# Splitting the late loads of v from those of q and k, and replacing the written order of engines and banks, in a fused attention and feed-forward kernel

## The chip, the cores and the metric

The kernel runs on one core of a Trainium2 chip. The metric is the device time of the program in microseconds (us); lower is better. The kernel before takes 197.51 us, the median of three runs (197.26 to 197.86).

## The reference

The inputs are q, k and v of shape (4 batches, 8 heads, 768 positions, 64), and two weights, w_in (512 x 2048) and w_out (2048 x 512). Attention keeps, for each query, the first 8 positions ("global") and the last 96 ("local"), with a distance penalty whose slope goes with the head. The result is laid out as 3072 tokens of 512 and goes through a feed-forward layer.

```
rel = pos[:, None] - pos[None, :]
keep = (pos[None, :] < 8) | ((rel >= 0) & (rel < 96))
scores = where(keep, q @ k.T / sqrt(64) - slope * dist, -1e9)
x = softmax(scores) @ v            # to (3072, 512)
out = relu(x @ w_in) ** 2 @ w_out  # (3072, 512), f32
```

## The kernel before

The tokens are cut into 24 tiles j of 128 rows (6 for each batch), and pairs of tiles form 12 blocks of 256 rows. A token tile goes through attention: q and k are transposed so that the head dimension lies on partitions (operations tr and T), the bias and the scores are made in PSUM (bias L597, sc L618), ScalarE takes exponentials (exp L684), VectorE multiplies them by a mask of decays (mul L709), TensorE multiplies with v, which carries a column of ones for the sum (pv L767), and VectorE divides by that sum (norm, a reciprocal at L797 and a product at L798). The first rows of k and v of a batch serve all its tiles; small copies, gk and gv (L455 on VectorE, L453 on ScalarE), put them where the next tile reads them. So x is made tile by tile, and then transposed: for the first 8 tiles by TensorE and a copy (trx L835, xT), for the other 16 by a transposing DMA on SP's queue (L859). Tiles 8 and up also have their q and k transposed by such DMAs (T.j on SP).

The feed-forward layer works on blocks. Block 0 and half of block 1 take the plain product (s1 L1081), with relu (L884 or L886) and square (sq). From there on each 256-row block and each half g of w_in uses a scheme of seven products in place of eight (h.blk.g.p1 to p7, L967): differences of x (xs, L939) and sums of w_in (isum, L907) feed it, ScalarE copies four of the results out of PSUM (u, L453), a custom VectorE instruction adds a PSUM bank to such a copy and clips at zero (c, L1011; c21 is a plain clip, L884 or L886), and a square follows (q, L1031 on ScalarE or L1033 on VectorE). The second layer has the same scheme: sums of the squared tiles (sum, L1185) and of w_out (wsum, L1150), seven products (s2.blk.p1 to p7, L1230), copies of parts (part), sums of two outputs of 128x256 (o, L1305), and stores (st, L1327, SP's queue).

All inputs come by DMAs that GpSimd's queue (POOL) issues: the first tiles of q, k and v and the weights one by one (ld.q.j, ld.k.j, ld.v.j, ld.win, ld.wout, L330), and tiles 6 to 23 as one operation load.j, which issues v, q and k in this order (L334). A load of tile j reuses a slot of a ring: v has 10 slots, q and k have 6 that hold the first tiles and 3 further ones. A load may start when the last readers of its slot are done; a tiny memset by VectorE (gate.j) passes on some of these waits.

Nothing in the kernel chooses the order at run time or at build time: the class Plan records every operation with its dependences, and its method run gives them out in the order of a long string, ORDER. A word of it is the name of an operation, #n for its n-th instance, @A or @V for ScalarE or VectorE where either can do it, and after a colon the PSUM banks (0 to 7), or the buffers of a ring, that it takes. Each engine, and each DMA queue, gets its instructions in this order, and semaphores are added where a dependence crosses engines. So the string fixes which operation stands behind which on each engine.

Of the kernel before, what the change touches and what calls it, by code (L numbers as in the profile page):

```python
# [57 lines left out]
tr.0.0:0 T.0.0@V tr.1.0:1 bias.0.0:23 T.1.0@V ld.q.1 ld.k.1 tr.0.1:4 T.0.1@V ld.q.2 ld.k.2 E0.1 ld.q.3 ld.v.0 ld.k.3  # L58
tr.1.1:5 T.1.1@A ld.v.1 sc.0.0 bias.1.0:6701 exp.0.1.0:0 sc.1.0 tr.0.2:4 exp.0.0.0 gk.1@A T.0.2@V exp.1.0.0:1 tr.1.2:5
T.1.2@V bias.2.0:3264 sc.2.0 exp.1.1.0 exp.1.1.1:3 ld.k.4 exp.1.0.1 ld.q.4 pv.0.1:5 tr.0.3:7 pv.0.0:1 ld.v.2 gk.2@A  # L60
exp.2.1.1:4 exp.2.0.0:5 exp.2.0.1 exp.2.1.0 tr.1.3:0 T.0.3@V T.1.3@V sc.3.0:4730 norm.0.0:0 norm.0.1 pv.1.0:6 tr.1.4:1
ld.q.5 pv.1.1:2 norm.1.0:1 norm.1.1 trx.0:5 exp.3.1.1:6 ld.k.5 gv.1@A ld.v.3 tr.0.4:0 T.1.4@V T.0.4@V xT.0@A:0 gk.3@V
trx.1:6 exp.3.0.1 exp.3.1.0:7 exp.3.0.0 ld.win.1.0 pv.2.0:2 pv.2.1:5 norm.2.0:0 norm.2.1 gv.2@V mul.3.0:8 sc.4.0:1037
exp.4.1.0:9 trx.2:2 ld.win.4.0 xT.1@A exp.4.1.1:a tr.1.5:4 tr.0.5:5 T.1.5@A exp.4.0.0 xT.2@A:1 mul.3.1:b pv.3.0:0
pv.3.1:6 T.0.5@A s1.0.1:7 norm.3.0:1 gk.4@V exp.4.0.1 norm.3.1 gv.3@A s1.0.1#2 trx.3:4 sc.5.0:0126 exp.5.0.1:c
exp.5.1.0:d s1.0.4:5 exp.5.1.1 E0.0 mul.4.0:e xT.3@V ld.v.4 mul.4.1:f ones.6 pv.4.0:3 s1.1.1:4 relu.0.4@V:2 exp.5.0.0
ld.win.3.0 s1.0.3:2 pv.4.1:1 relu.0.1@A:0 sq.0.1@A:0 gv.4@A s1.0.3#2 mul.5.1:1 s1.1.3:6 norm.4.0:0 norm.4.1 ld.win.2.0
ld.win.0.0 s1.0.0:5 relu.0.3@A:3 sq.0.3@A mul.5.0:5 gate.10 s1.0.2:0 trx.4:7 relu.1.1@A:4 sq.1.1@A:1 xs.1.0:0 ld.v.5
ld.win.2.1 pv.5.0:3 ld.win.0.1 pv.5.1:1 xs.1.1 ld.win.6.0 ld.win.7.0 ld.win.5.0 relu.1.3@A:7 norm.5.0:1 norm.5.1
ld.wout.3 s1.1.2:2 xT.4@A:2 relu.1.2@A:8 ld.wout.2 ld.wout.1 ld.wout.0 isum.0.0 s1.1.0:4 s1.0.2#2 trx.5:3 gate.14  # L70
xT.5@V relu.1.0@A:6 sq.1.2@A s1.0.0#2 xs.2.0:1 h.2.0.p1:1 sq.1.0@V sq.0.4@A u.2.0.1@A:b isum.3.0 sq.1.3@A xs.2.1
ld.wout.7 isum.0.1 s1.0.0#3 s1.0.6:6 gate.11 isum.1.0 isum.1.1 xs.1.2 s1.0.7:7 h.2.0.p2:2 c.2.0.c11:9 h.2.1.p1:3
relu.0.6@A:a ld.wout.6 ld.wout.5 ld.wout.4 u.2.1.1@A:e relu.0.7@A:c isum.3.1 s1.0.0#4 h.2.1.p5:4 s1.0.2#3 relu.0.0@A:f
h.1.1.p1:6 h.2.1.p2:7 u.1.1.1@A:0 isum.2.1 h.2.1.p6 u.2.1.2@A:d h.1.1.p2:2 c.1.1.c11:3 xs.2.2 c.2.1.c11:5 sq.0.0@A
s1.0.2#4 isum.2.0 h.1.1.p6 u.1.1.2@A:1 h.2.0.p6 u.2.0.2@A:4 h.2.1.p7 u.2.1.3@A:8 h.1.1.p7 h.2.0.p5:5 relu.0.2@A:6
u.1.1.3@A:2 h.2.0.p7 wsum.0.0 h.1.1.p5:2 u.2.0.3@A:7 c.2.1.c22:b wsum.1.0 sq.0.2@A gate.9 s1.0.5:7 h.2.1.p3 wsum.2.0
c.2.0.c22:f load.6 load.7 c.1.1.c22:0 sq.0.7@A relu.0.5@A:e sq.0.6@A sq.0.5@A load.8 c.2.1.c12:8 sum.0.2:0 sum.0.0
h.1.1.p4 h.2.0.p4 wsum.0.1 s2.1.p1.0:0 T.8 c.2.0.c21@A:6 h.2.0.p3 h.2.1.p4 s2.0.p1.0:7 h.1.1.p3 sum.0.1 s2.0.p2.0:4
q.1.1.c22@A q.1.1.c11@A s2.0.p1.1 q.2.1.c22@A:2 q.2.0.c11@A part.0.p1@A:0 c.1.1.c21@A:c s2.0.p2.1 s2.1.p1.1 wsum.1.1
s2.0.p6.0 s2.0.p6.1 c.1.1.c12:7 tr.1.6:1 tr.0.6:6 part.1.p1@A:1 q.1.1.c21@A s2.1.p2.0:2 q.2.1.c11@A sum.0.3 wsum.2.1  # L80
part.0.p6@A:2 o.0.p2:a c.2.1.c21@A:2 s2.1.p2.1 wsum.3.1 wsum.3.0 T.1.6@V s2.0.p7.0 s2.0.p7.1 gate.12 s2.0.p5.0
q.1.1.c12@A s2.0.p5.1 c.2.0.c12:e load.9 part.0.p7@A:3 q.2.1.c12@A T.0.6@A q.2.0.c22@A o.0.p5:d s2.0.p4.0 s2.0.p4.1
q.2.0.c12@A o.0.p4@A sum.1.0:1 s2.0.p3.0 tr.0.7:3 gate.13 sum.1.1 s2.0.p3.1 o.1.p2:0 o.0.p3 sum.1.2 T.0.7@A tr.1.7:1
sum.2.2:0 sum.1.3 sum.2.0 T.1.7@A q.2.0.c21@A s2.1.p6.0 s2.1.p6.1 q.2.1.c21@A part.1.p6@A:0 sc.6.0:567341 exp.6.1.0:3
load.10 gk.7@A exp.6.0.0 s2.1.p5.0 s2.1.p7.0 s2.1.p7.1 mul.6.0:b exp.7.0.0:9 exp.7.1.0 part.1.p7@A:3 s2.2.p1.0:6
s2.1.p5.1 sum.2.1 exp.7.0.1:1 exp.7.1.1 o.1.p5:c mul.7.0:5 s2.2.p1.1 pv.6.0:5 norm.6.0:0 s2.1.p4.0 s2.1.p4.1 o.1.p4@A
pv.6.1:7 s2.1.p3.0 sc.8.0:3415 exp.8.0.1:7 part.2.p1@A:1 pv.7.0:0 s2.1.p3.1 mul.7.1:8 norm.6.1 T.9 pv.7.1:7 norm.7.0:1
# [5 lines left out]
part.2.p7@A:3 q.3.0.c11@A h.3.0.p5:2 h.3.1.p2:1 c.3.1.c11:8 gv.8@V load.11 c.3.0.c22:7 h.3.1.p3 h.3.0.p4 c.3.0.c21@A:2
h.3.1.p4 c.3.1.c21@A:1 q.3.1.c11@A c.3.1.c12:6 s2.2.p5.0 pv.9.0:5 gk.9@V T.11 st.0.0 norm.9.0:1 q.3.1.c12@A
q.3.0.c22@A h.3.0.p3 pv.9.1:1 gv.9@A c.3.0.c12:e norm.9.1 s2.3.p1.0:0 s2.2.p5.1 sc.10.0:4752 exp.10.1.1:f h.4.0.p1:1
s2.2.p4.0 exp.10.1.0:3 s2.2.p4.1 q.3.0.c12@V s2.3.p1.1 sum.3.0:1 o.2.p5:b s2.2.p3.0 s2.2.p3.1 exp.10.0.1 exp.10.0.0
part.3.p1@A:0 sum.3.1 h.4.1.p1:2 s2.3.p6.0 o.2.p4@A mul.10.0:8 s2.3.p6.1 sum.3.2 pv.10.0:7 mul.10.1:9 o.2.p3 gk.10@A
xT.9 norm.10.0:0 xs.4.0:1 xs.4.1 h.4.1.p2:5 pv.10.1:4 q.3.1.c21@A q.3.0.c21@A part.3.p6@A:1 u.4.1.1@A:6 u.4.0.1@A:5
s2.3.p7.0 s2.3.p7.1 h.4.1.p6 u.4.1.2@A:7 norm.10.1 h.4.0.p6 u.4.0.2@A:e gate.18 sc.11.0:6374 exp.11.1.0:a exp.11.0.0
gv.10@V c.4.1.c11:3 part.3.p7@V:3 sum.3.3 xs.4.2 load.12 h.4.0.p2:5 T.12 exp.11.1.1:1 h.4.1.p7 s2.3.p4.0 mul.11.0:2  # L100
exp.11.0.1 c.4.0.c11:f u.4.1.3@A:8 mul.11.1:9 load.13 h.4.0.p7 h.4.1.p5:3 c.4.1.c22:6 s2.3.p2.0:6 pv.11.0:4
u.4.0.3@A:a norm.11.0:1 q.4.1.c11@A:1 h.4.1.p4 h.4.0.p5:7 c.4.0.c22:5 s2.3.p2.1 o.3.p2:2 pv.11.1:5 q.4.1.c22@A
h.4.1.p3 q.4.0.c11@A gate.16 norm.11.1 h.4.0.p4 c.4.1.c21@A:1 c.4.0.c21@A:3 h.4.0.p3 s2.3.p4.1 c.4.1.c12:8 q.4.1.c12@A
# [69 lines left out]
def kernel(  # L173
# [37 lines left out]
    NBIAS = 3  # L211
    JQK, JX = 8, 8
    JGATE = 9
    NQ, NKT, NV = 3, 2 * TPB, 10
    NBANK = 8
    G = ("bank", NBANK)

# [266 lines left out]
    for j in range(NT):  # L484
# [270 lines left out]
        for hf in range(2):  # L755
# [22 lines left out]
            if not first:  # L778
                deps.append(glob.get(("v", j - 1)))
# [670 lines left out]
```

## Time and profile before

| | us |
|---|---|
| median of three runs | 197.51 (197.26 to 197.86) |
| span of the profiled execution | 195.7 |
| what lies around the span (median less span; the profiled execution has no other time of its own) | 1.8 |
| PE (matmul) busy | 188.5, 2808 matmuls |
| VectorE busy | 179.4, 437 instructions |
| ScalarE busy | 161.6, 338 instructions |
| GpSimd (POOL) busy | 75.1, nearly all of it issues of loads |

The table is read from the first line of the profile. Instructions on an engine overlap a little: an engine starts one before the last has written its result, so the time from start to start is shorter than the duration. A busy TensorE is not yet a TensorE that sets the time; that is seen from the chain of work that ended last, and from what each engine waited for. In a timeline each line has the start, the time that the group of instructions takes, engine, line and operation, and in brackets the idle time in front of it with what ended it.

### The profile page before, as it was taken

The page shows a single profiled execution, that of the slowest core. Times are in us where ns is not written, and L with a number is a line of the kernel's source. Part 1 is how long each engine was busy: PE and PEld are TensorE (multiplying, and loading weights), DVE is VectorE, ACT ScalarE, POOL GpSimd, SP SyncE. Part 2 cuts the span into 40 slices and gives each one's busy share as a digit, 9 for nine tenths or more (in the row PEclk, how much of TensorE's full clock was granted, in tenths as well). Part 3 has the DMA queues.
Part 4 walks back from the last instruction along what each step waited for, and adds up shares of the span by engine and source line. Part 5 has one row for each costly group of instructions (what it writes and reads, how often), then busy time and mean ns, then how long its engine had stood idle before and what let it go on. Part 6 is the DMA issues. An engine that isn't in the chain of part 4 may idle for free.

```text
span 195.7 us, 6835 instructions
## 1 busy us (share of the span) xinstructions
PE 188.5 (96%) x2808; PEld 170.5 (87%) x2808; DVE 179.4 (92%) x437; ACT 161.6 (83%) x338; POOL 75.1 (38%) x93
## 2 busy tenths in 40 slices
PE   7986999999999999999999999999999999999993
PEld 3774999999888989989989989989889999999982
DVE  8569989999999999989999999899999899999982
ACT  6699999999989797999899997587987798986600
POOL 8999784775564502650047080119200000000000
PEclk9999999999999999999999999999999999999999
DMA  7999999999999999999949989999947440152026
GB/s 125 149 150 167 179 193 205 205 162 151 155 150 143 99 177 168 119 100 227 139 79 129 138 74 119 209 168 97 147 113 188 85 136 13 20 193 105 0 91 234
DMA packets 111713, 26.92 MB, mean 138 GB/s; under 512 B 103234, under 2 KB 108866, under 8 KB 111682
## 3 DMA queue, kind: packets, MB, share of 16 engines
q0 software_dynamic: 80256, 13.37, 91.9%
q1 hardware_dynamic: 31426, 13.11, 33.4%
q8 instruction: 22, 0.36, 0.7%
q14 instruction: 9, 0.07, 0.1%
HBM read 27.26 MB, written 6.29 MB: 171 GB/s over the span
## 4 chain that ended last, share of the span: by engine, by line
PE 85%; POOL 6%; DMA 5%; DVE 1%; issue 0%; POOLq 0%; DVEq 0%
PE bank L1230 37%; PE bank L967 32%; PE bank L1081 6%; PE bank L618 5%; PE bank L767 5%; POOL qk_first L330 5%; DMA win<-in_moe_w_in_dram 3%; DMA xT<-x 2%; POOL v L330 2%; PE bank L835 1%; PE bank L528 0%; DVE xs L939 0%; DVE buf L886 0%; DVE hsum L1185 0%; DVE early L1305 0%
## 5 line engine op out<-in xcount | busy, mean ns | idle before, releaser
L684 ACT ACTIVATE buf<-bank 128x512 bf16<-128x512 f32 x76 | 41.5, 613 | 2.8 <-PE bank L618 2.7
L1031 ACT ACTIVATE hs<-buf 128x512 bf16<-128x512 f32 x62 | 37.2, 635 | 2.5 <-DVE buf L1011 2.0
L1230 PEld LDWEIGHTS <-hsum 128*128 128x128 bf16 x384 | 35.3, 98 | 4.0
L453 ACT COPY buf<-bank 128x512 f32<-128x512 f32 (+1 forms) x59 | 32.1, 569 | 7.7 <-PE bank L967 6.1
L1230 PE MATMUL bank<-wsum,hsum 128*128 128x256 bf16 x288 | 38.0, 273 | 0.0
L1011 DVE CUSTOM_DVE_ANT_0 buf<-bank,buf 128x512 f32<-128x512 f32 x49 | 33.0, 682 | 0.8 <-ACT buf L453 0.3
L967 PEld LDWEIGHTS <-qk_first 128*128 128x128 bf16 x504 | 31.1, 98 | 1.4 <-issue 0.3
L967 PEld LDWEIGHTS <-win 128*128 128x128 bf16 x504 | 30.8, 98 | 0.9
L334 POOL DMA_DIRECT2D qk<-in_q_dram x18 | 16.0, 889 | 35.3 <-DMA qkT<-qk 30.0
L1230 PEld LDWEIGHTS <-hs 128*128 128x128 bf16 x288 | 26.3, 98 | 2.7
L1230 PE MATMUL bank<-wout,hs 128*128 128x256 bf16 x192 | 27.3, 273 | 0.0
L334 POOL DMA_DIRECT2D v<-in_v_dram x18 | 16.0, 891 | 23.1 <-PE bank L967 13.1
L967 PE MATMUL bank<-xs,qk_first 128*128 128x128 bf16 x336 | 24.6, 219 | 0.2 <-DVE buf L886 0.2
L967 PE MATMUL bank<-xT,win 128*128 128x128 bf16 x336 | 24.6, 219 | 0.0
L709 DVE TENSOR_TENSOR buf<-buf,E 128x1024 bf16<-128x1024 bf16 x32 | 21.5, 683 | 0.5 <-ACT buf L684 0.5
L798 DVE TENSOR_TENSOR x<-bank,rs 128x256 bf16<-128x256 f32 x48 | 20.4, 425 | 1.7
L767 PE MATMUL bank<-v,buf 128*128 128x65 bf16 x312 | 16.1, 193 | 0.9 <-DMA v<-in_v_dram 0.5
L1185 DVE TENSOR_TENSOR hsum<-hs 128x1024 bf16<-128x1024 bf16 (+1 forms) x26 | 16.4, 642 | 0.3
L334 POOL DMA_DIRECT2D qk<-in_k_dram x18 | 16.1, 897 | 0.6 <-DMA wout<-in_moe_w_out_dram 0.4
L767 PEld LDWEIGHTS <-buf 128*128 128x128 bf16 x312 | 13.9, 98 | 1.8 <-DVE buf L709 0.6
L884 ACT ACTIVATE buf<-bank 128x512 f32<-128x512 f32 x23 | 13.7, 607 | 1.0 <-PE bank L967 1.0
L453 ACT COPY part<-bank 128x256 f32<-128x256 f32 x29 | 11.1, 383 | 3.6 <-PE bank L1230 3.6
(92 smaller groups left out, 349.4 us busy)
## 6 DMA issues: line engine op xcount, KB each, us to landing
out_dram<-buf SPq DMA_DIRECT2D x17, 256.0 KB, 2.7
v<-in_v_dram POOLq DMA_DIRECT2D x24, 128.0 KB, 5.4
qk<-in_q_dram POOLq DMA_DIRECT2D x18, 128.0 KB, 5.0
qk<-in_k_dram POOLq DMA_DIRECT2D x18, 128.0 KB, 5.5
wout<-in_moe_w_out_dram POOLq DMA_DIRECT2D x8, 256.0 KB, 9.7
win<-in_moe_w_in_dram POOLq DMA_DIRECT2D x6, 256.0 KB, 7.1
out_dram<-early SPq DMA_DIRECT2D x5, 256.0 KB, 2.7
qk_first<-in_q_dram POOLq DMA_DIRECT2D x5, 128.0 KB, 4.6
```

Of the source, the lines that this page charges most:

```text
L334: nc.gpsimd.dma_start(out=dst, in_=src)
L453: nc.scalar.copy(dst, src)
L684: nc.scalar.activation(out=tiles[tag, j, g][:, odd], in_=tiles.pop(("sc", j, odd, g)).rearrange("p a c -> p (a c)"), func=Act.Exp, scale=s ...
L709: nc.vector.tensor_mul(at, tiles.pop(("esc", j, g)), bias)
L767: nc.tensor.matmul(out=po[:, hi, :], lhsT=tiles["at", j, g][:, odd, at * P : (at + 1) * P], rhs=v_sb[kj][:, h, :], start=(i == 0), stop=(i ...
L798: nc.vector.tensor_tensor(out=x[:, 4 * hf : 4 * hf + 4, :], in0=po[:, :, :D], in1=rs.to_broadcast([P, 4, D]), op=Alu.mult,)
L884: nc.scalar.activation(dst, src, Act.Relu)
L967: nc.tensor.matmul(out=tiles["h", blk, g, bank][:, n], lhsT=left_[:, s, k], rhs=right_[:, k], start=opens and n == 0 and k == 0, stop=k == ...
L1011: nc.vector._custom_dve(TENSOR_ADD_SAT, out=hr, in0=src, in1=tiles.pop(("u", blk, g, i)), s0=float("inf"), s1=0.0,)
L1031: nc.scalar.activation(hs, hr, Act.Square)
L1185: nc.vector.tensor_tensor(out=t[:, i, h], in0=t[:, a, h] if isinstance(a, int) else half_a(blk, *a)[:, h], in1=t[:, b, h] if isinstance(b, ...
L1230: nc.tensor.matmul(out=tiles["acc", blk, bank][:, cols], lhsT=left_[:, s], rhs=right_[:, cols], start=first and s == 0, stop=s == NSTEP - ...
```

## The change

Three things are edited. The operation load.j of a late tile becomes two, load.j.0 for v and load.j.1 for q and k, and each waits only for the readers of its own slots; the product pv then names the load of v of the tile before it as a dependence of its own. The eight PSUM banks become eight slices of one tile, and the two buffers of xs two halves of one tile. ORDER is replaced as a whole. Code for two further forms (a norm over both halves of a tile at once, WHOLE, and the seven products over a pair of blocks, PAIRS) is added, and both are switched off; the seven products of a single block stay as they were. The count of instructions and of DMAs on each engine that do work stays the same (2808, 437 and 338 on PE, VectorE and ScalarE), with a few copies and squares exchanged between VectorE and ScalarE; instructions that only wait for a semaphore go from 91 to 129 on VectorE and from 75 to 108 on ScalarE.

```diff
-    banks = [ps.tile([P, 4 * P], FP32, name=f"bank_{i}", tag=f"bank_{i}") for i in range(NBANK)]
+    bank_all = ps.tile([P, NBANK, 4 * P], FP32, name="bank", tag="bank")
+    banks = [bank_all[:, i] for i in range(NBANK)]
...
+    WHOLE = False
+    PAIRS = ()
+    NXT = 3
...
-            ("xT", 3, [P, KM, 2 * P], BF16), ("xs", 2, [P, 4, 2, P], BF16),
+            ("xT", NXT, [P, KM, 2 * P], BF16),
...
+    xs_all = const([P, 2, 4 * 2 * P], BF16, "xs")
+    buffers["xs"] = [xs_all[:, i].rearrange("p (z k c) -> p z k c", z=4, k=2) for i in range(2)]
...
-            def emit_load(e, j=j):
+            def emit_load_v(e, j=j):
                 load_v(j)
+
+            def emit_load_qk(e, j=j):
                 load_part(0, j)
                 load_part(1, j)
...
             ld = plan.op(
-                ("load", j), {"POOLQ": 2.6}, emit_load,
-                deps=qk_users[slot(j)] + v_users[j % NV] + [ones.get(j), gate], key=base, ready=issue[0],
-            )
+                ("load", j, 0), {"POOLQ": 0.88}, emit_load_v,
+                deps=v_users[j % NV] + [ones.get(j), gate], key=base, ready=issue[0],
+            )
+            land["v", j] = plan.op(("data", j, 0), {"DMAQ": 0.9}, None, deps=[ld])
+            ld = plan.op(
+                ("load", j, 1), {"POOLQ": 1.75}, emit_load_qk,
+                deps=qk_users[slot(j)], key=base, ready=issue[0],
+            )
+            land["q", j] = land["k", j] = plan.op(("data", j, 1), {"DMAQ": 1.8}, None, deps=[ld])
...
             if not first:
-                deps.append(glob.get(("v", j - 1)))
+                deps += [glob.get(("v", j - 1)), land["v", j - 1]]
```

The two orders, up to the first scores of tile 5 (engines and banks are left out here, and so are bias, exp and the smaller operations; loads are cut to their tile):

```
before: tr.0.0 tr.1.0 q1 k1 tr.0.1 q2 k2 q3 v0 k3 tr.1.1 v1 sc.0 sc.1 tr.0.2 tr.1.2 sc.2 k4 q4 pv.0
        tr.0.3 v2 tr.1.3 sc.3 pv.1 tr.1.4 q5 trx.0 k5 v3 tr.0.4 gk.3 trx.1 win1 pv.2 gv.2 sc.4 trx.2 win4
        tr.1.5 tr.0.5 pv.3 s1.0.1 gk.4 trx.3 sc.5
after:  tr.0.0 tr.1.0 k1 tr.1.1 q1 tr.0.1 sc.1 gk.1 q2 tr.0.2 k2 tr.1.2 v0 sc.0 sc.2 k3 tr.1.3 q3 q4 tr.0.3
        gk.2 tr.0.4 pv.0 sc.3 v1 k4 pv.1 gv.1 trx.0 tr.1.4 v2 pv.2 sc.4 trx.1 v3 pv.3 trx.2 k5 tr.1.5 q5
        tr.0.5 win3 trx.3 sc.5 s1.0.3
```

The late loads stand in the order before as load 6, 7, 8, 9, 10, 11, 12, 13, 15, 14, 16, 17, 19, 20, 18, 22, 21, 23. After, the halves go 6.1 8.1 7.1 7.0 6.0 9.1 8.0 15.0 10.1 13.0 11.1 11.0 9.0 10.0 12.1 13.1 14.1 16.0 15.1 12.0 16.1 17.1 14.0 17.0 18.1 19.1 20.1 19.0 18.0 22.1 20.0 21.1 23.1 21.0 22.0 23.0.

More of the change, by code (lines that the diff above doesn't have):

```diff
@@ L78 @@
[L78 to L87, printed above, removed]
@@ L93 @@
[L93 to L102, printed above, removed]
@@ L1058, in group @@
             hidden_part("c12", "z", p3, 2, 0, 1)
-        for g in groups:
+        for g in range(4) if wide else groups:
             group(g)
```

344 lines of the change are left out of this document (200 added, 144 removed).

## The prediction

> **What bounds the kernel now.** Read the page first (busy shares, granted clock, chain), then the stretches of the span, then the chain piece by piece.
>
> ```profile
> PE 188.5 (96%) x2808; PEld 170.5 (87%) x2808; DVE 179.4 (92%) x437; ACT 161.6 (83%) x338; POOL 75.1 (38%) x93
> PEclk9999999999999999999999999999999999999999
> PE 85%; POOL 6%; DMA 5%; DVE 1%; issue 0%; POOLq 0%; DVEq 0%
> ```
> ```profile
> 20.00:50.00 30.00, 30.00 (x434) 28.29 (x431) 28.76 (x69) 28.57 (x58) 19.97 (x25) 1.00 1.75 181
> 50.00:70.00 20.00, 20.00 (x322) 18.09 (x319) 19.40 (x48) 17.52 (x39) 10.52 (x12) 1.00 1.85 136
> 70.00:130.00 60.00, 59.81 (x944) 55.15 (x943) 56.79 (x137) 52.76 (x111) 18.41 (x21) 1.00 1.37 140
> 130.00:170.00 40.00, 40.00 (x629) 36.84 (x626) 38.46 (x88) 34.59 (x73) 6.99 (x8) 1.00 0.75 108
> ```
> ```profile
> 123.03 4.44 DMA xT<-x
> 128.31 0.60 DVE hsum L1185
> 128.91 0.61 DVE buf L886
> ...
> 182.77 9.64 PE bank L1230 x88
> ```
>
> TensorE ends last nearly everywhere, at full granted clock. In the second fence the columns are the stretch, its length, then busy time of PE, PEld, DVE, ACT and POOL. From 20 to 170 us PE is never seen idle for more than 0.19 us of a stretch, and VectorE follows close: 28.76 + 19.40 + 56.79 + 38.46 = 143.41 of 150, so it has only 6.6 us of idle time (4.4%). ScalarE has 17%. So the time is PE's work plus PE's waits. The chain leaves PE twice: in the head, for loads, and at 123 to 129.5 us, for a late transpose of x and two VectorE operations.
>
> The yardstick for both orders is the **offset**: the time at which PE starts an operation less the PE work put ahead of it. The work is counted from start-to-start spacings: 88 matmuls of the second layer in 9.64 us are 0.1095 each, and likewise for the others. Where PE waits, the offset rises; nothing lowers it again.
>
> ```profile
> 15.77 0.65 PE L767 MATMUL bank<-v,buf 128*128 128x65 bf16 x16 [0.49 <-DMA v<-in_v_dram]
> 16.35 0.23 PE L618 MATMUL bank<-qkT 64*128 64x128 bf16 x2
> ...
> 18.40 0.40 PE L767 MATMUL bank<-v,buf 128*128 128x65 bf16 x8 [0.21 <-ACT buf L684]
> 18.98 0.42 PE L767 MATMUL bank<-v,buf 128*128 128x65 bf16 x8 [0.17 <-DVE buf L709]
> 19.66 1.07 PE L1081 MATMUL bank<-xT,win 128*128 128x128 bf16 x16 [0.27 <-DMA win<-in_moe_w_in_dram]
> 20.56 0.39 PE L835 MATMUL bank<-ident,x 128*128 128x128 bf16 x4
> 20.88 0.23 PE L618 MATMUL bank<-qkT 64*128 64x128 bf16 x2
> ```
>
> At 19.66 the first product with w_in has 10.91 us of PE work ahead of it (offset 8.75), at 20.88 sc.5.0 has 12.02 (8.86). The rest of the span adds 0.9: the offset is 9.07 near 60 us of work, 9.2 up to 115, 9.62 after the wait that ends at 129.5, and 9.77 at the end (the chain's last piece of PE ends at 182.77 + 9.64 = 192.41, after 182.6 of PE work). Those 9.77 us are all that a new order can win or add to; PE's 2808 matmuls and their shapes are the same in both kernels.
>
> **The change part by part.** *Loads split.* Late loads of v, q and k were one operation of the order and become two (v; q and k); the same 88 transfers on the POOL queue, and none added. What it removes is a wait:
>
> ```profile
> POOL qk L334 <- DMA qkT<-qk: 30.0, 6, 9.9
> POOL v L334 <- PE bank L967: 13.1, 1, 13.1
> ```
>
> POOL waited 43 us in these two rows alone (total, times, longest), yet PE's waits in the trace name loads only in the head, where the loads are single already. Late loads are early enough before; earlier ones bring **0**. The cover is this slack of many us; if a load came late, it would cost PE the lateness. *Banks as one tile, differences of x as one tile with two halves, written-out sizes*: the same memory and the same instructions: **0**. The branches for wide pairs and whole norms are switched off.
>
> *The order of the head (to about 20 us).*
>
> ```profile
> L330 POOL DMA_DIRECT2D win<-in_moe_w_in_dram x10: 740/882/940, 13.6 to 23.4; - x10
> ```
> ```profile
> win<-in_moe_w_in_dram POOLq DMA_DIRECT2D x6, 256.0 KB, 7.1
> ```
> The new list asks for v2 as 11th load and for its first w_in piece as 15th, just as before, so both land as before: v2 lets PE go on at 15.77, w_in at 19.66. PE work ahead of the first pv that needs v2: 8.61 before, 8.38 new, so this landing costs 0.23 more there. Ahead of the first w_in product: 10.91 before, 11.78 new, so that landing, which set 8.75, sets only 19.66 − 11.78 = 7.88. What is late next is the chain of copies and exps between: from 16.35 to 20.88 PE did 2.92 us of work (sc.4.0 up to sc.5.0) in 4.53, so 1.61 of waits. In the new order the work between these two is 2.26 and the same pieces are on the way (a copy of the transposed k on ScalarE behind x's copy, gv.2, two exps, T.0.5 on VectorE behind four norms). Starting sc.4.0 at 16.3 to 17.1 and adding 2.26 and 0.9 to 1.6 of waits gives sc.5.0 at 19.5 to 20.9, middle 20.1, with 11.13 ahead: offset 8.4 to 9.8, middle 8.97. The last w_in piece, issued at 23.4 and 7.1 on its way, has 22.7 of PE work ahead of its user in the new order: 23.4 + 7.1 − 22.7 = 7.8, which binds nothing. Against 8.86: I take **+0.1** (−0.4 to +0.9).
>
> *VectorE from there on.* Its spacings:
>
> ```profile
> 16.21 0.18 DVE L797 RECIPROCAL rs<-bank 128x4 f32<-128x4 f32 x1
> ...
> 16.77 0.17 DVE L797 RECIPROCAL rs<-bank 128x4 f32<-128x4 f32 x1
> ```
> ```profile
> 58.94 0.41 DVE L455 COPY xT<-bank 128x512 bf16<-128x512 bf16 x1
> 59.27 0.41 DVE L1305 TENSOR_TENSOR early<-bank,part 128x256 f32<-128x256 f32 x1
> ...
> 60.29 0.67 DVE L455 COPY v<-v 8x520 bf16<-8x520 bf16 x1
> ```
> ```profile
> 125.76 1.28 DVE L1011 CUSTOM_DVE_ANT_0 buf<-bank,buf 128x512 f32<-128x512 f32 x2
> 127.55 0.42 DVE L939 TENSOR_TENSOR xs<-xT 128x512 bf16<-128x512 bf16 x1 [0.52 <-DMA xT<-x]
> 128.01 0.29 DVE L939 TENSOR_TENSOR xs<-xT,xs 128x256 bf16<-128x256 bf16 x1
> 128.22 0.68 DVE L1185 TENSOR_TENSOR hsum<-hs,hsum 128x1024 bf16<-128x1024 bf16 x1
> ```
> A pair of two customs takes 1.28, so one follows the other after 0.60, and the 0.6 holds for muls, sums and squares; a norm with its reciprocal takes 16.77 − 16.21 = 0.56; a sum of two outputs 0.33; a small xs 0.21. Count now what VectorE must have done between two operations of PE that wait for it. Before: from c.3.0.c12 (for sc.10.0) to norm.22.1 (for s2.9.p2.0) stand 39 customs, 24 muls, 24 sums, 7 squares, 3 plain copies, 27 norms, 21 outputs and small ones: 87.6 us beside 93.55 of PE work, spare 6.0. New: from mul.10.0 (for pv.10.0) to c.10.0.c21 (for h.11.1.p1) 43 customs, 24 muls, 24 sums, 9 squares, 28 norms, 20 outputs: 90.7 beside 94.73, spare **4.0**. Squares and customs are taken over earlier and from ScalarE. With 6.0 spare, PE lost 9.77 − 9.07 = 0.7 over this stretch. If losses go with the inverse of the spare, 0.7 × 6.0 / 4.0 = 1.05, **+0.35**. Half of the 0.7 is the one event at 123 to 129.5, which the new order doesn't hold in that place (pv.17.1 and the first use of that transpose stand 9.1 us of work apart). So the low end is −0.35; the high end is where the queue stays late: VectorE idled 4.4% over 150 us, and were it to need the same share in the new stretch, 4.2 of 94.73 against 4.0, hardly more; with 1% more, 0.95: to +1.3 with the 0.35.
>
> *Added waits.* VectorE gets 38 more instructions that only wait, ScalarE 33.
>
> ```profile
> L455 DVEq EVENT_SEMAPHORE  x12: 21/21/50, 9.9 to 157.1; - x12
> ```
> At 21 ns those are 0.8 us in VectorE's queue, if nothing hides them. An operation of 0.68 us there starts the next after 0.60, so the queue runs ahead by 0.08, more than 21 ns; I take **0** (0 to +0.3 on PE, since not all of VectorE is on the path).
>
> *Copies beside POOL's issues.*
>
> ```profile
> L455 DVE COPY v<-v x8: 280/304/669, 17.3 to 166.6; 8x520 bf16<-8x520 bf16 x8
> L455 DVE COPY qkT<-qkT x7: 152/165/606, 15.5 to 162.4; 128x32 bf16<-128x32 bf16 x7
> ```
> ```profile
> 59.94 0.90 POOL L334 DMA_DIRECT2D v<-in_v_dram  x1
> ```
> The copy of global v at 60.29 took 0.67 against 0.28 at least, with POOL issuing a load from 59.94; the longest copy of global k took 0.606 against 0.152. The head is full of such issues (w_in's alone go from 13.6 to 23.4). Before, three of these copies are on VectorE there (gk.3, gk.4, gv.2), new five (gk.1, gk.2, gv.1, gv.3, gv.4): 2 × 0.4 = 0.8 us more on VectorE, of which the head's +0.9 end already holds what reaches PE. The Trainium skill ("SBUF — State Buffer", section "SBUF: two separate sides") has VectorE's two-port operations and GpSimd share one pair of ports as an exclusive lock, so that the later one blocks until the other is done. By that rule the two extra copies would wait for up to one issue each, and gk.2 stands right ahead of what sc.3.0 needs; the rows at 59.94 and 60.29 agree with it, and the rule speaks against this change.
>
> *The tail*: the last product ends the same way (one 128x256 output, one 128 KB store), **0** (±0.1).
>
> **Sum**: +0.1 + 0.35 + 0 + 0 = about +0.4. The profiled execution's span of 195.7 would become 196.1; the median of the runs shown, 197.51, stands 1.8 above the span for what lies around it, so 197.9.
>
> **The rivals.** *Faster, 196.5*: w_in no longer holds PE at 8.75, the head ends at the low end of the walk (−0.4), and the late transpose with the waits around it goes (−0.35), with nothing in its place: 197.5 − 0.75, or 1.0 with the small waits. For it: these waits are in the trace. Against it: spare 4.0 instead of 6.0. *VectorE becomes the bound, 198.9*: from the point where VectorE must idle more than 4.0 of 94.73 us, that is 4.3%, each further us of idle time goes to PE; before it idled 4.4%. At 1% more, 0.95 + 0.35 = 1.3. For it: the share is at the edge. Against it: idle time can shrink as a queue fills, since a late engine finds its inputs ready. *Copies blocked in the head, 198.7*: two copies longer by 0.4, and one issue behind, on PE at sc.3.0 and sc.5.0: +0.9 instead of +0.1. For it the row at 60.29, against it that VectorE has gaps in the head. *A late transpose elsewhere, 198.4*:
>
> ```profile
> xT<-x SPq DMA_TRANSPOSE x16, 2.7
> ```
> The new order leaves 4.6 us of PE work between pv.18.1 and h.9.0.p1; norm 0.56, landing 2.7 and the pv 0.25 need 3.5, and the chain above had a 4.44. If VectorE is 1 us late, PE waits 0.5 or more. *The change doesn't do what it says*: loads stay hidden whenever they are issued, and the split moves nothing; it is contained in the forecast.
>
> **How the numbers follow.** Forecast within 0.3% of before (what a measurement of this kernel can tell from no change), near 197.9: 0.40. Faster rival 0.22; VectorE bound 0.22; copies in the head 0.09; late transpose 0.07. Faster than 196.9: 0.22; same: 0.38, since the forecast's own high end passes 198.1; slower: 0.40. The range 196.7 to 199.1 takes in most of the faster case and the VectorE case, leaving 1 in 10 on each side; the forecast alone would be 197.2 to 198.6.
>
> **What would show it.** Right: an offset of 8.7 to 9.1 after sc.5.0, no PE wait for win before it, no PE wait for a late load, VectorE above 96% from 50 to 170 us, and PE's waits behind c, mul or xs on VectorE. Wrong: an offset near 8.4 at 30 us that stays below 9.4 to the end (faster); VectorE at 98% with PE losing over 1.5 us between 60 and 160 (bound); copies of global k and v of 0.6 in the head ahead of PE waits.

## The result, and the profile after

The changed kernel is slower: 199.05 us at the median of 20 runs (197.84 to 204.32) against 197.56 for the kernel before in runs on the same chip (20 runs, 196.94 to 199.35). The ratio is 1.0061, with a 95% interval of 1.0032 to 1.009, so about 1.2 us with an interval of 0.6 to 1.8. Two of the 20 (201.6 and 204.32) count as slow executions and stay out of the ratio; the other 18 lie between 197.84 and 200.79. The profiled execution took 198.13 us with a span of 196.3; its time was among the shortest of the 20.

The page of the changed kernel, the two lines that answer to those shown of before:

```profile
PE 188.8 (96%) x2808; PEld 170.8 (87%) x2808; DVE 178.1 (91%) x437; ACT 160.2 (82%) x338; POOL 75.1 (38%) x93
...
PE 85%; DMA 4%; DVE 4%; ACT 4%; issue 1%; POOL 1%; ACTq 0%; DVEq 0%; POOLq 0%
```

The work of each engine is nearly what it was. In the chain the loads of the head (POOL 6% before, 1% now) have given way to VectorE (1% before) and ScalarE (not in the row of before), 4% each; transfers have 4%, where they had 5%. The stretches of the changed kernel (length, then busy time of PE, PEld, DVE, ACT, POOL):

```profile
20.00:50.00 30.00, 29.98 (x448) 28.06 (x448) 29.04 (x70) 27.44 (x56) 20.99 (x27) 1.00 1.70 184
50.00:70.00 20.00, 19.94 (x324) 17.71 (x319) 19.38 (x46) 19.41 (x45) 10.41 (x12) 1.00 2.26 148
70.00:130.00 60.00, 60.00 (x966) 56.54 (x963) 57.83 (x140) 53.37 (x111) 20.71 (x24) 1.00 1.46 147
130.00:170.00 40.00, 39.97 (x617) 36.49 (x615) 38.41 (x91) 33.27 (x71) 3.83 (x5) 1.00 0.86 112
```

Busy shares say little here: VectorE has 144.66 of 150 us (29.04 + 19.38 + 57.83 + 38.41) against 143.41 before. The offset of TensorE (its start of an operation less the PE work ahead of it) says where the time went. It is worked out from the matmuls of each trace as in the prediction; another choice of the spacings moves a step between two columns by some 0.05:

| PE work ahead, us | 16 | 52 | 84 | 131 | 152 | end |
|---|---|---|---|---|---|---|
| before | 8.77 | 8.82 | 9.21 | 9.64 | 9.68 | 9.78 |
| changed | 8.73 | 9.13 | 9.64 | 9.77 | 10.08 | 10.35 |

The end stands 0.57 us higher, which is the 0.6 us between the spans. From 16 to 52 us of work the new order loses 0.40 where the old one lost 0.05. From 52 to 84 it loses 0.51 against 0.39. From 84 to 131 it loses 0.13 against 0.43, so it wins 0.30, for the late transpose of x that cost the kernel before 0.35 is gone. Behind that it loses 0.58 against 0.14.

Places of these losses in the timelines of the changed kernel (start, time, engine, line, operation; L1022 is the L967 of before, L1282 the L1230, L777 the L767):

```profile
45.36 0.69 DVE L1202 TENSOR_TENSOR wsum<-wout 128x1024 bf16<-128x1024 bf16 x1
```
```profile
63.35 0.71 DVE L455 COPY v<-v 8x520 bf16<-8x520 bf16 x1
63.98 1.27 DVE L715 TENSOR_TENSOR buf<-buf,E 128x1024 bf16<-128x1024 bf16 x2
```
```profile
63.09 0.88 POOL L334 DMA_DIRECT2D qk<-in_q_dram  x1 [4.11 <-DMA qkT<-qk]
```
```profile
190.59 0.42 DVE L1357 TENSOR_TENSOR early<-bank,part 128x256 f32<-128x256 f32 x1 [0.44 <-DMA out_dram<-early]
```

The first line is the sum wsum.2.1. It ends at 46.05 and TensorE starts the product that needs it at 46.10, 0.18 late. The copy gv.8 takes 0.71 us beside an issue of GpSimd that runs from 63.09 to 63.97; the two muls behind it are late by that, and TensorE loses 0.41 from 65 to 68. At the end VectorE waits 0.44 for a store of block 9 to be done with the buffer that the last outputs use, and TensorE loses 0.23.

That explains 0.6 of the 1.2 us, in one execution. The spread of the times (197.84 to 200.79) asks for more.

### The profile page after: what moved, and what is told of

The parts are those of the page before. It is cut to its first block, busy times and chain, and to the rows that moved or that the text cites. A ratio compares the mean times of both kernels' runs of the same rounds, so it can differ in the third digit from the quotient of the medians.

```text
span 196.3 us, 6913 instructions
## 1 busy us (share of the span) xinstructions
PE 188.8 (96%) x2808; PEld 170.8 (87%) x2808; DVE 178.1 (91%) x437; ACT 160.2 (82%) x338; POOL 75.1 (38%) x93
## 4 chain that ended last, share of the span: by engine, by line
PE 85%; DMA 4%; DVE 4%; ACT 4%; issue 1%; POOL 1%; ACTq 0%; DVEq 0%; POOLq 0%
PE bank L1282 35%; PE bank L1022 32%; PE bank L1143 5%; PE bank L624 5%; PE bank L777 5%; DMA qk_first<-in_q_dram 2%; DMA out_dram<-early 2%; DVE x L836 1%; ACT early L690 1%; ACT buf L690 1%; PE bank L534 1%; PE bank L873 1%; DVE buf L715 1%; POOL qk_first L330 1%; DVE rs L835 0%
## 5 line engine op out<-in xcount | busy, mean ns | idle before, releaser
L1089 ACT ACTIVATE hs<-buf 128x512 bf16<-128x512 f32 x54 | 33.8, 648 | 6.9 <-DVE buf L1067 6.9
L1282 PEld LDWEIGHTS <-hsum 128*128 128x128 bf16 x384 | 35.3, 98 | 4.8 <-issue 0.4
L1282 PE MATMUL bank<-wsum,hsum 128*128 128x256 bf16 x288 | 39.0, 273 | 0.0
L690 ACT ACTIVATE buf<-bank 128x512 bf16<-128x512 f32 x62 | 35.0, 627 | 0.9 <-PE bank L624 0.5
L1022 PEld LDWEIGHTS <-win 128*128 128x128 bf16 x504 | 30.7, 98 | 0.6
L1022 PEld LDWEIGHTS <-qk_first 128*128 128x128 bf16 x504 | 30.6, 98 | 0.7
L1282 PEld LDWEIGHTS <-hs 128*128 128x128 bf16 x288 | 26.7, 98 | 2.9
L1067 DVE CUSTOM_DVE_ANT_0 buf<-bank,buf 128x512 f32<-128x512 f32 x41 | 27.5, 685 | 0.5 <-ACT buf L453 0.2
L1282 PE MATMUL bank<-wout,hs 128*128 128x256 bf16 x192 | 25.9, 273 | 0.0
L334 POOL DMA_DIRECT2D qk<-in_q_dram x18 | 16.1, 893 | 23.7 <-DMA qkT<-qk 19.4
L1022 PE MATMUL bank<-xT,win 128*128 128x128 bf16 x336 | 24.0, 219 | 0.0
L1022 PE MATMUL bank<-xs,qk_first 128*128 128x128 bf16 x336 | 23.8, 219 | 0.0
L690 ACT ACTIVATE early<-bank 128x512 bf16<-128x512 f32 x26 | 15.2, 613 | 1.8 <-PE bank L624 1.8
L922 ACT ACTIVATE buf<-bank 128x512 f32<-128x512 f32 x20 | 12.1, 608 | 4.3 <-PE bank L1022 1.7
L715 DVE TENSOR_TENSOR buf<-buf,E 128x1024 bf16<-128x1024 bf16 x23 | 15.3, 681 | 0.0
L453 ACT COPY early<-bank 128x512 f32<-128x512 f32 (+1 forms) x14 | 7.9, 565 | 7.4 <-PE bank L1282 6.0
L1282 PE MATMUL bank<-wsum,hs 128*128 128x256 bf16 x96 | 13.6, 273 | 0.0
```

Source lines behind the costliest of these rows:

```text
L334: nc.gpsimd.dma_start(out=dst, in_=src)
L453: nc.scalar.copy(dst, src)
L690: nc.scalar.activation(out=tiles[tag, j, g][:, odd], in_=tiles.pop(("sc", j, odd, g)).rearrange("p a c -> p (a c)"), func=Act.Exp, scale=s ...
L715: nc.vector.tensor_mul(at, tiles.pop(("esc", j, g)), bias)
L922: nc.scalar.activation(dst, src, Act.Relu)
L1022: nc.tensor.matmul(out=tiles["h", blk, g, bank][:, n], lhsT=left_[:, s, k], rhs=right_[:, k], start=opens and n == 0 and k == 0, stop=k == ...
```

## The experiments

**Theories.** A: the new order puts the work of VectorE and ScalarE such that TensorE always waits, by the same 0.3 to 0.4 us in each execution. B: it brings many transfers (transposes, stores, loads) to land just when they are used, and as a transfer's time differs from execution to execution, now one and now another is late. C: VectorE's copies within SBUF are held up by GpSimd's issues, also by chance of position. The rival of all three: the code itself (split loads, tiles) costs or gains something.

The edits of the order below name the words that move. A transfer has as much time "in hand" as lies between its landing and its first use.

**order_before**: the changed program with the order of before.

```diff
-load.6 load.7 ...
+load.6.0 load.6.1 load.7.0 load.7.1 ...
```

> The changed program (split loads, banks and differences as slices of one tile) with the order of before; each split load stands as its two halves, one behind the other, in the old place. If the order is all that costs: the time of the kernel before within 0.15%, and the waits of TensorE that the trace of before shows, with no wait of TensorE for a transposing transfer or behind a store. If the slices of one tile or the halves cost something: 0.3% or more slower.

Measured: 197.45 us, ratio 1.0005 (0.998 to 1.0029). The program is not the cause; the order is. Even the count of waiting instructions is that of before (91 on VectorE), so the 38 more came with the order. Its trace is a second execution of the old order, with offsets of 8.87, 8.92, 8.99, 9.54, 9.57 and 9.67 in the columns above. The copy gv.7, which in the trace of before took 0.67 us, stands here as

```profile
60.40 0.28 DVE L461 COPY v<-v 8x520 bf16<-8x520 bf16 x1
```

and TensorE lost 0.03 us there, where it had lost 0.24. The same copy at the same place in the order costs in one execution and not in the other. The late transpose of x was there again:

```profile
129.45 0.61 PE L1028 MATMUL bank<-xs,qk_first 128*128 128x128 bf16 x8 [0.29 <-DVE buf L930]
```

**after_same**: the changed kernel once more, nothing edited.

> The changed kernel once more, for a second trace and the spread of its times. Its profiled execution had a span of 196.3 us, the profile of the kernel before 195.7. Theory A (queues of VectorE and ScalarE between 33 and 68 us, fixed by the order): each execution loses the same 0.3 to 0.4 us there, and the median stays 0.5 to 0.7 us above the kernel before. Theory B (transfers at the edge: the late store of block 9 that a buffer of the last output waits for, the late transposes of tile 23): the executions differ by 1 us and more, the extra time stands in front of the last outputs or of sc.23.0, and the median stays 1.0 to 1.5 us above before.

Measured: 198.41 us (197.53 to 199.73), ratio 1.0029 (0.9996 to 1.0063). The profiled execution took 199.06 us, 0.9 more than the first one, and its losses stand elsewhere. In the head (VectorE, then POOL), where the first execution had 0.17 and 0.36 for the same two copies:

```profile
13.00 0.73 DVE L457 COPY qkT<-qkT 128x32 bf16<-128x32 bf16 x1
...
16.39 0.60 DVE L457 COPY v<-v 8x520 bf16<-8x520 bf16 x1
```
```profile
12.73 1.00 POOL L332 DMA_DIRECT2D qk_first<-in_q_dram  x1
```

The copy gk.2 starts at 13.00 and ends at 13.73, in the moment in which the issue ends (12.73 + 1.00). The offset at 16 us of work is 9.53 in place of 8.73. And near the end TensorE waits for a transposing transfer of k (tile 23) that the first execution had 0.19 us in hand:

```profile
150.78 0.23 PE L626 MATMUL bank<-qkT 64*128 64x128 bf16 x2 [0.73 <-DMA qkT<-qk]
```

So B and C are both seen. So is a loss as A has it: from 16 to 52 us of work this execution lost 0.39, the first one 0.40, and in both some 0.17 of it stands at wsum.2.1. The median is between what A (0.5 to 0.7 us above before) and B (1.0 to 1.5) had asked for and nearer to A: 0.8 us above the kernel before in the medians, 0.6 by the ratio.

**tail_buffer**: another buffer for the last outputs.

```diff
-o.11.p5:1
+o.11.p5:e
```

> The changed kernel with another buffer for the last outputs of block 11 (buffer e, whose last reader is a square at 183 us, in place of buffer 1, from which the store of block 9 is still being read at 190 us). If that store is what holds the end (theory B, tail): 0.2 to 0.25 us less in a run like the profiled one, 0.5 us or more at the median if the store's time varies, and no wait of VectorE for a store near the end. If the end is set by the second product alone: within 0.1 us of the changed kernel.

Measured: 198.52 us, ratio 1.0042 (1.0019 to 1.0065). The wait at the end is gone: in this trace the same output follows a copy with no wait for a store,

```profile
191.16 0.42 DVE L457 COPY part<-bank 128x256 f32<-128x256 f32 x1
191.69 0.42 DVE L1359 TENSOR_TENSOR buf<-bank,part 128x256 f32<-128x256 f32 x1
```

and the offset doesn't rise over the last 30 us by more than 0.04 (0.27 before the edit). That is worth 0.2 us, too little for these times to show, and less than theory B had wanted from the tail. The rest of the execution was worse than both others: it lost 0.41 and 0.57 us for two transposes of q and k (tiles 9 and 11) that had 1.9 and 3.1 us in hand in the first one, 0.57 for the store st.1.1 (the case of the next run) and 0.29 for the transpose of x of tile 20:

```profile
59.10 0.23 PE L626 MATMUL bank<-qkT 64*128 64x128 bf16 x2 [0.34 <-DMA qkT<-qk]
```
```profile
69.09 0.23 PE L626 MATMUL bank<-qkT 64*128 64x128 bf16 x2 [0.51 <-DMA qkT<-qk]
```
```profile
88.50 1.09 ACT L692 ACTIVATE buf<-bank 128x512 bf16<-128x512 f32 x2 [0.73 <-DMA out_dram<-buf]
```
```profile
89.64 0.55 PE L1024 MATMUL bank<-xT,win 128*128 128x128 bf16 x7 [0.42 <-ACT buf L692]
```

**gv8_early**: the copy gv.8 ahead of two customs.

```diff
-norm.8.1 ... c.3.1.c11:b h.3.0.p2:5 c.3.0.c11:7 gv.8
+norm.8.1 gv.8 ... c.3.1.c11:b h.3.0.p2:5 c.3.0.c11:7
```

> The changed kernel with the copy of global v of tile 8 moved ahead of two custom instructions on VectorE, so that it runs at about 62.0 us, when GpSimd issues nothing, in place of 63.35, where it took 0.71 us beside an issue that began at 63.09. If the copy is blocked until the issue ends (theory C): 0.28 to 0.3 us long, mul.9.0 ends 0.4 earlier, and the offset of TensorE at 68 us is 9.2 to 9.4 in place of 9.6, 0.2 to 0.4 us less in all. If the length of the copy has another reason: still 0.6 to 0.7 long, and no gain.

Measured: at its place, as theory C had it:

```profile
61.88 0.29 DVE L457 COPY v<-v 8x520 bf16<-8x520 bf16 x1
62.09 1.27 DVE L1069 CUSTOM_DVE_ANT_0 buf<-bank,buf 128x512 f32<-128x512 f32 x2
```

The copy is 0.29 long, and the offset at 68 us of PE work is 9.10 (9.6 before the edit). But the whole was 199.35 us, ratio 1.0081 (1.0049 to 1.0113), so no gain. This execution lost 0.81 us in one place, for ScalarE waited for the store st.1.1 to be done with a buffer (ACT, then PE):

```profile
87.70 1.57 ACT L692 ACTIVATE buf<-bank 128x512 bf16<-128x512 f32 x3 [1.08 <-DMA out_dram<-buf]
```
```profile
88.84 0.55 PE L1024 MATMUL bank<-xT,win 128*128 128x128 bf16 x7 [0.65 <-ACT buf L692]
```

In the first trace the same store landed at 86.99, just in time for that operation to start at 87.07 with no loss on TensorE.

**store_early**: st.1.1 ahead in SP's queue.

```diff
-T.13 st.0.0 ... xT.11 st.2.0 st.1.1
+T.13 st.1.1 st.0.0 ... xT.11 st.2.0
```

> The changed kernel with one store moved: st.1.1, whose data is ready at 60 us, goes to SP's queue ahead of the store of block 0, at about 73 us in place of 81. In three of four executions so far it landed at 87.0 to 88.4 and held the first exponential of tile 14, and the 0.6 to 0.95 us that TensorE lost at 89 us followed. Theory B: that loss is gone in the trace, and the median is 0.2 to 0.6 us lower. If something else is late there: the loss stays, with another releaser.

The expectation counts three executions of four with a loss at 89 us. In their traces the store landed at 86.99 to 88.42 and held ScalarE in three, but TensorE lost time in two, tail_buffer and gv8_early.

Measured: the wait is gone in the trace, and the offset at the end is 9.90, nearly that of the kernel before. But the median was 199.69 us, ratio 1.0092 (1.0064 to 1.012): the expectation of a lower median failed. The profiled execution took 198.56 us in spite of its low offset; its very last store took 2.70 us to land, where the other traces show 1.7.

**margins**: four places given room at once.

```diff
-load.15.0 load.10.1 ... load.13.0 load.11.1 ... load.10.0
+load.10.1 ... load.11.1 ... load.10.0 load.13.0 load.15.0
```

and the edits of tail_buffer, gv8_early and store_early.

> The changed kernel with four places given room at once: st.1.1 early, another buffer for the last outputs, the copy gv.8 ahead of two customs, and the loads of v of tiles 13 and 15 (used at 91 and 106 us) behind those of q and k of tiles 10 and 11, which the split had let them pass, so that the transposes of tiles 10 and 11 can go out 0.9 and 1.8 us earlier. Theory B with C: 0.7 to 1.3 us less than the changed kernel at the median, so within 0.3 us of the kernel before, spread halved; what stays is the head and the transposes of tile 23. If the cost is the length of the queues of VectorE and ScalarE (theory A): 0.2 to 0.4 us less only.

Measured: 199.11 us (197.87 to 205.63), ratio 1.0047 (0.9998 to 1.0096). Neither the ratio nor the spread came down as expected. In its trace the four places are quiet and others are late, the transpose of x of tile 9 above all (VectorE, then PE):

```profile
74.46 0.42 DVE L993 TENSOR_TENSOR xs<-xT 128x512 bf16<-128x512 bf16 x1 [0.84 <-DMA xT<-x]
```
```profile
75.27 0.62 PE L1024 MATMUL bank<-xs,qk_first 128*128 128x128 bf16 x8 [0.56 <-DVE xs L993]
```

**late_group**: the transposing transfers of tiles 18, 19, 20 and 23 earlier.

```diff
-st.4.0 ... xT.16:1 ... st.3.0 st.4.1 xT.17 T.18 T.19 ... T.20 load.20.0 load.21.1 ... T.22 T.21 ... load.23.1 xT.19 T.23
+st.4.0 T.18 ... xT.16:1 T.19 T.20 ... st.3.0 st.4.1 xT.17 ... load.20.0 load.21.1 load.23.1 ... T.22 T.21 T.23 ... xT.19
```

> The changed kernel with the transposing transfers of q and k of tiles 18, 19, 20 and 23 and the load of q and k of tile 23 put earlier in the queues (the first three to about 109 to 113 us in place of 117 to 121, the last to about 130 in place of 143), and nothing else. In six executions of such orders T.23 landed within 0.3 us of the scores that use it, and xT.20 behind it within 0.05 us in two. Theory B: no wait of TensorE for either in the trace, 0.1 to 0.9 us less from execution to execution, 0.3 to 0.5 at the median. If those places don't matter for the median: the same time as the changed kernel within 0.2 us.

Measured: 201.76 us, ratio 1.0176 (1.0128 to 1.0224), so slower than the kernel before by 1.3 to 2.2%, and slower than the changed kernel. The transfer of tile 23 now lands 16 us ahead of its use, as meant. But the earlier transposes freed their slots earlier, GpSimd issued nine loads one behind the other from 116.08 to 123.95, and into these fell the transpose of x of tile 17 (SP's issue, the loads, VectorE, PE):

```profile
117.41 1.95 SPq L899 DMA_TRANSPOSE xT<-x  x1
```
```profile
116.08 1.75 POOL L336 DMA_DIRECT2D v<-in_v_dram  x2 [14.42 <-PE bank L1024]
```
```profile
124.91 0.42 DVE L993 TENSOR_TENSOR xs<-xT 128x512 bf16<-128x512 bf16 x1 [2.72 <-DMA xT<-x]
```
```profile
125.72 0.95 PE L1024 MATMUL bank<-xs,qk_first 128*128 128x128 bf16 x14 [1.98 <-DVE xs L993]
```

It landed some 7.5 us after its issue (117.41 to 124.9). In the changed kernel, with two loads issued beside it, it took 2.4 (115.54 to 117.95). This is the clearest case of the study: a transfer is not a fixed time, and moving one moves the loads behind it. That it was the loads that held this transpose up is read from what ran beside it; no run has the one without the other.

**room**: late_group, the loads of v and the buffer as above, gv.8 early, st.1.1 ahead of xT.11 and st.0.1 behind xT.13. This kernel computes part of the output wrong; which of the moves does that is not known, so its time is read only for where TensorE waited.

> The changed kernel with room at all places that I know: the late transposes as in late_group; the store st.1.1 ahead of the transpose of x of tile 11 (at about 77.5 us in place of 81); the loads of v of tiles 13 and 15 behind those of q and k of tiles 10 and 11; gv.8 ahead of two customs; another buffer for the last outputs; one store behind the transpose of x of tile 13. Theory B with C: the offset at the end is 9.5 to 9.9 in most executions, the median within 0.3 us of the kernel before or below it, and the spread like that of before (nine in ten within 1.2 us). If after this it is still 0.7 us or more above before, what makes the changed order slower is not at these places, and the theory that single late transfers carry the difference is wrong or lacks its main part.

Measured: 200.72 us, ratio 1.0149 (1.0104 to 1.0194), far above what was expected. The 1.65 us that TensorE lost at 108 us is of my own making: st.0.1, put back by one place, held an exponential.

```profile
107.74 0.60 ACT L692 ACTIVATE buf<-bank 128x512 bf16<-128x512 f32 x1 [1.88 <-DMA out_dram<-buf]
```
```profile
108.39 0.40 PE L779 MATMUL bank<-v,early 128*128 128x65 bf16 x8 [1.48 <-ACT buf L692]
```

That doesn't explain all of it. If every execution lost these 1.65, the median without them would be 199.1, still 1.5 us above the kernel before on the same chip (197.59), and the expectation had named 0.7 as the point from which the theory of single late transfers is wrong or lacks its main part. Held to that, the theory is not confirmed. With a wrong output, and with the transpose of x of tile 17 late here too (VectorE waited 0.75 for it), the run doesn't refute it either.

**loads_joined** and **joined_gates**: the split undone within the new order, v directly ahead of its q and k; in the second with all the tiny memsets (gate) as early as the readers of v allow.

```diff
-load.12.1 T.12 ... gate.12 ... load.12.0
+gate.12 load.12.0 load.12.1 T.12 ...
```

> The changed kernel with the split of the late loads undone: each v issued directly ahead of its q and k, at the place of q and k, with four of the tiny memsets that pass on waits moved ahead where that needs it. My prediction has the split at nothing: within 0.3 us of the changed kernel, though issues fall elsewhere beside VectorE's copies (0.4 us either way at most). The rival that the split pays for itself, or costs, gives a change of 0.5 us or more and a wait of TensorE for a load or for a transposing transfer.

> The split undone once more, as in loads_joined (v issued directly ahead of its q and k), but now with every tiny memset that passes on a wait standing as early as the readers of v allow. If loads_joined was slow because those memsets stood late in VectorE's order: most of the 25 us gone, and GpSimd no longer waits 20 us for one. If it was slow because v itself waits for its slot and holds q and k behind it: still 5 us or more above the changed kernel, with GpSimd waiting for readers of v. If the split is worth nothing: within 0.5 us of the changed kernel.

Measured: 223.68 us, ratio 1.1279 (1.1222 to 1.1335), and 204.43 us, ratio 1.029 (1.0235 to 1.0345). My expectation for the first failed by 25 us. GpSimd stood for a memset that came late in VectorE's order, with the load of q and k of tile 12 behind it, and, in a second row, for TensorE to be done with a slot of v (16.7 of it ahead of the load of v of tile 19):

```profile
POOL v L336 <- DVE v L506: 27.2, 2, 20.8
POOL v L336 <- PE bank L1024: 22.4, 2, 16.7
```

With the memsets early most of that is gone, but 2.9% stays, some 5 us above the changed kernel, with GpSimd still waiting once for ScalarE's copy of v and once for a memset:

```profile
POOL v L336 <- ACT v L455: 5.9, 1, 5.9
POOL v L336 <- DVE v L506: 5.8, 1, 5.8
```

So in the new order the split is not worth nothing: the order is built on it. In the old one, with the halves one behind the other, it is worth nothing (order_before).

**before_swap** and **before_two**: what the traces say of the kernel before, tried on it.

```diff
-T.20 xT.17
+xT.17 T.20
```

and in before_two also

```diff
-gv.7@V h.3.0.p2:7 ... xs.3.0:0 xs.3.1
+h.3.0.p2:7 ... xs.3.0:0 xs.3.1 gv.7@V
```

> The kernel before with two neighbours on SP's queue exchanged: the transpose of x of tile 17, which VectorE and then TensorE waited for (0.35 and 0.46 us lost in two executions, the transfer taking 4.4 us), ahead of the transposing transfer of q and k of tile 20, which nothing needs for 20 us. Alone, such a transpose of x takes 2.4 us. If a transfer is slow because of what is in flight ahead of it: it lands 1 to 2 us earlier, the loss at 129 us is gone, and the time is 0.3 to 0.45 us below the kernel before (197.1). If it is slow because of the loads that land at the same time: no change.

> before_swap, and in addition the copy gv.7 behind the two differences of x on VectorE, out of reach of the issue of the load of v that ends at 60.84 us. In one execution of this order the copy took 0.67 us and TensorE lost 0.24 us at 61 to 63 us, in another it took 0.28 and TensorE lost 0.03. Theory C: 0.28 long, and no loss there in any execution; 0.1 us below before_swap on average, below what the times can show.

Measured: 196.93 us, ratio 0.9973 (0.9946 to 0.9999), and 196.91 us, ratio 0.9989 (0.9962 to 1.0016). TensorE's loss at 129 us shrank, to 0.12 and 0.22 in these two executions from 0.35 and 0.46 in before and order_before, and so did VectorE's wait (0.28 in before_swap, 0.52 in before):

```profile
126.86 0.43 DVE L939 TENSOR_TENSOR xs<-xT 128x512 bf16<-128x512 bf16 x1 [0.28 <-DMA xT<-x]
```

but not for the reason that I gave: the transpose still took 4.2 us from issue (122.56 to 126.77) with the transfer of tile 20 behind it, against 4.4. What is in flight ahead of it does not explain its length. In before_two the copy gv.7 took 0.28, as theory C had it, and TensorE lost nothing there:

```profile
61.31 0.28 DVE L455 COPY v<-v 8x520 bf16<-8x520 bf16 x1
```

But this execution lost 0.52 from 16 to 52 us of work, at 32.6 and 49.6 us, far from both edits and where the other three of the old order lost 0.05. The first of the two intervals ends just under 1, the second does not exclude 1; that the exchange makes the kernel before faster by some 0.2% is not settled. Both beat the changed kernel.

## Why the prediction was right or wrong

The range of 196.7 to 199.1 held the median of 199.05 barely. The forecast of 197.9 did not come true; the direction, slower, had 0.40. That the number lies in the range is in good part luck: its high end was there for VectorE as the bound and for blocked copies in the head. VectorE did not become the bound, the copies cost time in one execution and not in the next, and late transfers, which had 0.07, made up much of the rest. The time follows the offset, as the prediction had it: in ten of the eleven profiled executions worked out (the changed kernel, order_before, after_same, tail_buffer, gv8_early, margins, late_group, room, before_swap, before_two) the time is the offset at the end plus 187.6 to 187.8 us. Only store_early stands at 188.7, by its last store. So the offset was the right thing to forecast. Of its terms some were mis-sized, one had the wrong mechanism, and one was missing.

- *Loads split, 0.* Right for the program, whose ratio alone is 1.0005. The reason given for the cover was too short: the prediction looked at TensorE waiting for a load, and late loads are followed by a transposing transfer and then by the scores. In the new order that chain had 0.19 us in hand at tile 23, and there it ran dry.
- *The head, +0.1 (−0.4 to +0.9).* w_in no longer holds TensorE, as said. The offset behind the head was 8.62 to 9.53 over six executions of the new order and its small edits (after_same, tail_buffer, gv8_early, store_early, margins and the first), against 8.77 and 8.87: a mean of 8.9, near the term, and a spread inside its bounds.
- *Copies beside POOL's issues.* The rival was right as a mechanism and wrong as an alternative: it isn't this or that for a kernel, but for an execution. Over twelve traces (all but loads_joined and joined_gates), each of the 95 copies gk and gv on VectorE with no issue of POOL beside it took 0.15 to 0.17 (gk) or 0.28 to 0.31 us (gv); of 85 with one beside it 51 took longer than 0.20 or 0.31, up to 0.75 and 0.71, and 49 of these ended with the issue or up to 0.12 behind it. gv8_early shows it by an edit, for one place. The Trainium skill ("SBUF — State Buffer", section "SBUF: two separate sides") calls the pair of ports that VectorE and GpSimd share an exclusive lock, with the later one blocked for the whole instruction of the other; the copy of 13.00 to 13.73 that ends with the issue agrees with that.
- *VectorE from there on, +0.35.* This step failed. It had the loss grow with the inverse of VectorE's spare time between 60 and 160 us. Over that stretch of work the changed kernel lost 0.54 (9.54 to 10.08) and the kernel before 0.66 (9.07 to 9.73), though VectorE had less idle time. The loss came earlier: 0.39 to 0.41 from 16 to 52 us in each execution without a late transfer there, 0.05 in three of four of the old order (theory A). In each of the new order some 0.17 of it stands at wsum.2.1 and 0.08 at 33.4 to 34.3 us; the rest is spread thin. That A's 0.35 is the size of the term is chance: the place and the reason are others.
- *Added waits, 0.* Nothing in the traces speaks against it; it wasn't tried by itself.
- *The tail, 0 (±0.1).* Wrong by 0.23: the last outputs take a buffer that a store issued 3.5 us before is reading. The prediction had looked at the last operations, not at who holds their buffers.
- *Stores* were missing: the prediction counted transposes and loads that could come late, but no store that holds a buffer (st.1.1, st.9.1).
- *A late transpose elsewhere, 0.07.* The place named (tile 18, 4.6 us of work) had 1.1 us in hand and never cost anything; tiles 9, 11, 20 and 23 did, now one, now another. The chance was too small because each place was looked at by itself. A list of the transfers that an engine used within 0.1 us of their landing has two names in two executions of the old order (xT.17 and once a store) and seven in six executions of the new one and its small edits (xT.9, xT.13, xT.20, T.9, T.11, T.23, st.1.1). Six executions give more names than two, so the list shows that the places change, not that there are more of them in one execution: behind the head, transfers made an engine wait 0.08 us or more 1, 2, 1 and 2 times in the four of the old order, and 1, 3, 4, 1, 1 and 2 times in the six.

The sizes: theory A gives 0.35 in every execution, 0.40 less 0.05. From 52 us of work to the end the new order and its small edits lost 1.22, 1.38, 1.92, 1.57, 0.58 and 1.75, in the mean 1.40, and the old one 0.96 and 0.75; that leaves 0.5 for B and C on average, and most of the scatter. By the steps of the offset at single waits, late transfers make some 0.8 of the 1.40 and 0.4 of the old order's 0.86, so most of these 0.5 is B. Together 0.9, between the ratios of the two sets of runs of the changed kernel (1.0061 and 1.0029, which is 1.2 and 0.6 us). Four of the six executions are of edited orders, and the edits themselves took some waits away.

What stays open: that the order is the cause is shown by order_before. That late transfers carry a good part of the difference is read from the executions that were traced. It is not shown that giving them room brings the time back: every attempt (tail_buffer, store_early, margins, late_group, room) took away the waits that it aimed at and came out no faster beyond the noise; in the traces of margins, late_group and room other transfers were late instead. No edit tried theory A, as by putting wsum.2.1 earlier. Why the medians of store_early and gv8_early lie above the changed kernel's, no trace here says. And why one transfer takes 4.8 us in one execution and 8.0 in another (xT.20) was not tried.

## What to carry to other kernels

An order is not only as good as its queues in one execution: list for every transfer (loads, transposes and stores that hold a buffer) how long before its use it lands, and compare that with how much its time differs between two executions. Where many have less in hand than that, the waits of one trace name only those that happened to be late, and taking these away, one by one or four at once, brought nothing here. Before a transfer is moved, ask what its end sets free: the loads that it lets start may slow the next one.

## What the runs showed of the hardware

The time from issue to landing of a transposing transfer goes with the order of the issues around it, and differs between executions. For the transposes of x, the minimum, median and maximum in us of one execution, first before, then changed:

```profile
DMA to landing us min/median/max: 2.4/2.7/5.5
```
```profile
DMA to landing us min/median/max: 2.4/4.0/8.1
```

and for those of q and k, before and then changed:

```profile
DMA to landing us min/median/max: 3.1/5.2/6.7
```
```profile
DMA to landing us min/median/max: 4.3/6.2/8.4
```

The 32 transposes are the same in both. The changed program with the order of before (order_before), x's and then those of q and k, is back where before was:

```profile
DMA to landing us min/median/max: 2.4/2.7/6.2
```
```profile
DMA to landing us min/median/max: 3.1/4.6/6.8
```

The median of x's was 2.6 to 2.8 in four executions of the old order (with before_swap and before_two) and 4.0 to 4.4 in eight of the new one and its edits, so the order alone moves it. One and the same transfer took, over six executions of the new order and its small edits, 4.8 to 8.0 us (xT.20), 7.3 to 9.1 (T.11), 5.8 to 7.3 (T.9), 5.9 to 9.1 (the load of v of tile 12).

A small copy within SBUF on VectorE often ends only with the issue of GpSimd that it falls into (49 of 85 with an issue beside them, above), and at other times isn't lengthened at all. VectorE's 128x1024 bf16 products and sums were not lengthened: over the same twelve traces 597 with an issue beside them took 0.66 to 0.69 us, and 591 without one 0.67 to 0.69. In the kernel before, with the issue of 59.07 to 59.97 and the next one beside it:

```profile
59.69 0.69 DVE L709 TENSOR_TENSOR buf<-buf,E 128x1024 bf16<-128x1024 bf16 x1
```

It took 0.69, the mean of all of its kind being 0.683.
